# A list scheduler with PSUM banks owned by one engine at a time, four h banks in the last block, and low words of the weights scaled on ScalarE

## The chip, the cores and the metric

The kernel runs on one core of one Trainium2 chip. The core has five engines with queues of their own: TensorE (PE in the rows; PEld is its weight load), VectorE (DVE), ScalarE (ACT), GpSimd (POOL) and SyncE (SP). The metric is the device time of one execution in microseconds (us); smaller is better.

## What is computed

Banded attention over 4 batches, 8 heads, 576 positions and a head width of 64 feeds two multilayer perceptrons, each 512 to 2048 to 512 over 2304 tokens. Cut to what matters, the reference is:

```python
scores = np.where(mask, scale * q @ k.T + bias, -1e9)      # mask: 0 <= i - j < 128
attn = softmax(scores)
x = attn @ v                                              # 2304 x 512
h = x @ w_in
P = a[0] + a[1]*h + a[2]*h*h + a[3]*h*h*h
Q = 1 + abs(b[0])*abs(h) + abs(b[1])*h*h
x = (P / (Q + 1e-6)) @ w_out                              # first perceptron
h = x @ w2_in
return (h * (1 / (1 + np.exp(-h)))) @ w2_out              # second perceptron
```

## The kernel before

All data lie transposed, features on the partitions and tokens along the free axis. Products of fp32 are made as three matmuls of high and low parts: hi x hi, hi x lo and lo x hi. So each operand comes as a pair (xh and xl, gh and gl, the two parts of w and wo), of which the high part is a rounded copy ("cast", L447 on ScalarE, L451 on VectorE, L455 on GpSimd) and the low part a subtraction (L462 on VectorE, L466 on GpSimd).

**Weights.** The weights lie in DRAM as 64-bit floats. Each of 64 raw weight tiles (16 each of w1, wo1, w2 and wo2) is loaded as pairs of 32-bit words and made into fp32 by three operations on 128x512: an activation on the top words (L541, ScalarE), a shift of the low words to the right by 29 bits (L543, VectorE), and a shift-and-or of both (L545, VectorE).

**First stage, to about 551 us.** The 18 token tiles of 128 are worked in five blocks of 4, 4, 3, 4 and 3 tiles. There are 80 steps, one for each block and each of 16 hidden slices f. Blocks 0 and 1 run first with f 0 to 9 (block 0, then block 1), then with f 10 to 15; blocks 2, 3 and 4 follow whole. A step makes h in one PSUM bank by 12 matmuls (L844 to L846, in two halves), then evaluates the rational function on it: |h| and a linear form on ScalarE (L860, L866), den on VectorE (L874), its absolute value on ScalarE (L877), the numerator on VectorE (L878, L879), logarithm and exponential on ScalarE (L881, L883; the exponential is written back into the h bank), and three more operations on VectorE (L885, L887, L889). L889 is the last to read the h bank. Then come gh and gl, and 12 matmuls into four accumulators, acc0 to acc3 (L913 to L915), which run two steps behind (LAG 2). There are two h banks, four acc banks and two banks for the attention, atA and atB: eight in all.

The attention runs in 20 groups (5 blocks x 4 pairs of heads) between those steps: scores (L674, PE), mask (L680) and maximum (L687) on VectorE, exponential (L691, ScalarE), normalisation (L716 on ScalarE in block 0, L710 on GpSimd later), transposes (L730, PE), copies ph of the transposes out of PSUM (ScalarE, or GpSimd at L760, or VectorE at L767 and L771), and the product with v (L799, PE), whose result is split into xh and xl (L811) and is the block's input.

Beside this run the sums and splits of the second perceptron's weights (sums_w, sums_wo, st_w, st_wo), and spills of block 0's split weights to DRAM, which later blocks load again.

**Second stage, from about 551 us.** The second perceptron is computed in three groups of six token tiles with seven products in place of eight. Phase A (L1183 to L1185) makes h and the SiLU, phase B (L1249 to L1251) the output. Phase A's inputs are seven forms of x (xf; sums xs of 128x768), which are made during phase B of the group before (xf, xs at L462 or L466). Phase B's inputs xh_b and xl_b are made of g as it runs.

**Order.** Nothing here is ordered by hand. Each operation is recorded with a priority, one or more engines that may take it, and a cost (`Plan.op`); `Plan.schedule` is a list scheduler that simulates the engines and emits the program in the order that it found. `OPT` holds the options and priority offsets, `SHIFTS` a table (first operation, count, offset) that shifts priorities. `LATENCY` is the planner's time between an operation's end on one engine and its use on another. GpSimd and those VectorE operations that have no PSUM operand share a `port` in the plan. While PE has nothing to do at the program's start, dummy matmuls ("spin", L491) fill the planned gap.

## Time and profile before

| | us |
|---|---|
| median of 3 runs | 917.33 (916.65 to 919.83) |
| profiled execution | 920.78 |
| its span in the trace | 918.7 |

| engine | busy us | share of the span | instructions |
|---|---|---|---|
| PE | 875.1 | 95% | 5072 |
| DVE | 700.7 | 76% | 1382 |
| POOL | 618.9 | 67% | 591 |
| ACT | 583.5 | 64% | 1253 |

The span is what the trace covers; the execution's own time is 2.1 us longer. An engine's busy share is an average over stages with different limits, so the rows below go by stage. In the rows of a timeline the columns are start and duration in us, engine, line, operation, output<-inputs, sizes, count, and in brackets the idle time ahead of it with what ended it. In the groups by line, the numbers behind the first bar are total busy us and mean ns of one, behind the second the idle us ahead and what ended it.

### The profile page before, as it was taken

What the parts mean: (1) busy time and instruction counts of PE and PEld (TensorE: products, weight loads), DVE (VectorE), ACT (ScalarE), POOL (GpSimd) and SP (SyncE); (2) the same over time, 40 slices, a digit from 0 to 9 for tenths busy, and PEclk for the clock granted to TensorE, in tenths of its full rate; (3) what the DMA queues carried; (4) which work ended last, traced back from release to release, by engine and by line L of the source; (5) the groups of instructions that cost most, each with busy time, mean ns of one, the idle gap of its engine ahead of it and who ended that gap; (6) DMA issues with size and microseconds to landing.
All of it is one profiled execution on the core that took longest, in us unless ns stands there. A gap on an engine that the chain in (4) does not pass through costs nothing.

```text
span 918.7 us, 15313 instructions
## 1 busy us (share of the span) xinstructions
PE 875.1 (95%) x5072; PEld 769.7 (84%) x5072; DVE 700.7 (76%) x1382; ACT 583.5 (64%) x1253; POOL 618.9 (67%) x591
## 2 busy tenths in 40 slices
PE   8879899999999999999998999999999999999998
PEld 6647667877777888777777989999899998999998
DVE  5789988789999989999998985449843389533662
ACT  5878888689887788878777775336323365233441
POOL 2255655454767779778788776559954499645895
PEclk8989999999999999999999999999999999999999
DMA  7645585367798879757796888988788898788884
GB/s 238 252 133 165 197 273 165 137 199 275 234 340 260 252 243 307 243 192 239 239 345 221 286 266 303 325 296 285 239 279 256 264 307 256 250 270 253 249 269 167
DMA packets 80606, 228.94 MB, mean 249 GB/s; under 512 B 8464, under 2 KB 17168, under 8 KB 80528
## 3 DMA queue, kind: packets, MB, share of 16 engines
q1 hardware_dynamic: 78224, 219.58, 73.3%
q10 hardware_dynamic: 2304, 8.39, 2.3%
q8 instruction: 40, 0.66, 0.3%
q14 instruction: 38, 0.31, 0.1%
HBM read 178.65 MB, written 49.28 MB: 248 GB/s over the span
## 4 chain that ended last, share of the span: by engine, by line
PE 55%; DVE 15%; POOL 10%; ACT 10%; DMA 6%; issue 3%; SPq 0%; POOLq 0%; ACTq 0%; DVEq 0%
PE h L844 4%; PE z_a L1183 4%; PE z_a L1185 4%; PE z_a L1184 4%; PE h L845 3%; PE h L846 3%; POOL xf L466 3%; DVE t L874 3%; PE acc L913 3%; PE acc L915 2%; PE acc L914 2%; ACT t L866 2%; PE z_b L1249 2%; PE z_b L1251 2%; PE z_b L1250 2%
## 5 line engine op out<-in xcount | busy, mean ns | idle before, releaser
L913 PE MATMUL acc<-gh,wo 128*128 128x512 f32 (+1 forms) x320 | 121.4, 379 | 1.0 <-ACT x L447 0.8
L915 PE MATMUL acc<-gl,wo 128*128 128x512 f32 (+1 forms) x320 | 118.3, 370 | 2.7 <-POOL gl L466 2.6
L914 PE MATMUL acc<-gh,wo 128*128 128x512 f32 (+1 forms) x320 | 118.1, 369 | 0.4 <-POOL wo L466 0.4
L447 ACT CAST xh_b<-g 128x384 fp32r<-128x384 f32 x137 | 68.5, 514 | 78.7 <-PE z_b L1251 36.2
L462 DVE TENSOR_TENSOR xl_b<-g,xh_b 128x384 fp32r<-128x384 f32 x75 | 99.3, 1364 | 22.3 <-ACT xh_b L447 19.0
L466 POOL TENSOR_TENSOR gl<-t,gh 128x512 fp32r<-128x512 f32 (+1 forms) x80 | 98.5, 1231 | 22.6 <-ACT gh L447 15.6
L466 POOL TENSOR_TENSOR xl_b<-g,xh_b 128x384 fp32r<-128x384 f32 x93 | 107.6, 1172 | 3.8 <-ACT xh_b L447 1.2
L844 PE MATMUL h<-xh,ws 128*128 128x512 f32 (+1 forms) x256 | 97.0, 379 | 11.3 <-DVE t L889 11.2
L846 PE MATMUL h<-xh,ws 128*128 128x512 f32 (+1 forms) x256 | 93.0, 363 | 0.0
L845 PE MATMUL h<-xl,ws 128*128 128x512 f32 (+1 forms) x256 | 92.9, 363 | 0.0
L366 ACT ACTIVATE g<-t_a 128x384 f32<-128x384 f32 x72 | 37.8, 525 | 84.2 <-DVE t_a L359 84.2
L874 DVE SCALAR_TENSOR_TENSOR t<-t,ab,h 128x512 f32<-128x512 f32 (+1 forms) x80 | 55.3, 691 | 22.6 <-ACT t L866 20.0
L913 PEld LDWEIGHTS acc<-gh,wo 128*128 128x128 f32 x320 | 60.1, 188 | 13.8 <-issue 4.5
L915 PEld LDWEIGHTS acc<-gl,wo 128*128 128x128 f32 x320 | 60.1, 188 | 11.7 <-POOL gl L466 4.1
L844 PEld LDWEIGHTS h<-xh,ws 128*128 128x128 f32 x256 | 48.0, 188 | 25.3 <-DVE t L889 17.9
L466 POOL TENSOR_TENSOR g<-g,g 128x384 f32<-128x384 f32 x57 | 64.6, 1142 | 3.9 <-DVE xl_b L462 1.5
L914 PEld LDWEIGHTS acc<-gh,wo 128*128 128x128 f32 x320 | 60.1, 188 | 8.1 <-POOL wo L466 1.5
L860 ACT ACTIVATE t<-h,ab 128x512 f32<-128x512 f32 (+1 forms) x80 | 51.2, 641 | 23.4 <-PE h L846 22.9
L691 ACT ACTIVATE e<-e,m 128x128 f32<-128x128 f32 x144 | 56.2, 391 | 13.8 <-DVE m L687 13.5
L1183 PE MATMUL z_a<-xf,w2s 128*128 128x384 f32 x192 | 64.2, 334 | 0.4 <-DVE t L889 0.4
L1249 PE MATMUL z_b<-xh_b,wo2s 128*128 128x384 f32 x192 | 64.1, 334 | 0.0
L1251 PE MATMUL z_b<-xh_b,wo2s 128*128 128x384 f32 x192 | 64.1, 334 | 0.0
(178 smaller groups left out, 2736.1 us busy)
## 6 DMA issues: line engine op xcount, KB each, us to landing
w2s<-forms_w SPq DMA_DIRECT2D x84, 512.0 KB, 4.5
wo2s<-forms_wo SPq DMA_DIRECT2D x84, 512.0 KB, 4.6
ws<-sc SPq DMA_DIRECT2D x64, 512.0 KB, 4.8
raw_w<-in_w SPq DMA_DIRECT2D x32, 512.0 KB, 4.9
raw_wo<-in_wo SPq DMA_DIRECT2D x32, 512.0 KB, 4.6
forms_w<-st_w SPq DMA_DIRECT2D x24, 512.0 KB, 5.5
...
```

Of the source, the lines that this page charges most:

```text
L462: nc.vector.tensor_tensor(out=o, in0=a, in1=b, op=op)
L466: nc.gpsimd.tensor_tensor(out=o, in0=a, in1=b, op=op)
L844: nc.tensor.matmul(o, lhsT=T[W][:, 0, c], rhs=xh, start=kt == 0, stop=False)
L845: nc.tensor.matmul(o, lhsT=T[W][:, 0, c], rhs=xl, start=False, stop=False)
L846: nc.tensor.matmul(o, lhsT=T[W][:, 1, c], rhs=xh, start=False, stop=kt == KD - 1)
L874: nc.vector.scalar_tensor_tensor(out=t("t1"), in0=t("t2"), scalar=ab[:, 0:1], in1=hp_(), op0=ALU.add, op1=ALU.mult)
L913: nc.tensor.matmul(a, lhsT=T[WO][:, 0, c], rhs=T[G1][:, :n], start=first_f, stop=False)
L914: nc.tensor.matmul(a, lhsT=T[WO][:, 1, c], rhs=T[G1][:, :n], start=False, stop=False)
L915: nc.tensor.matmul(a, lhsT=T[WO][:, 0, c], rhs=T[G2][:, :n], start=False, stop=last_f)
L1183: nc.tensor.matmul(o, lhsT=w(0, kt * P), rhs=x[:, 0, kt], start=st and kt == 0, stop=False, skip_group_check=True)
L1249: nc.tensor.matmul(o, lhsT=w(0, m * P), rhs=h, start=st and q == 0, stop=False, skip_group_check=True)
L1251: nc.tensor.matmul(o, lhsT=w(1, m * P), rhs=h, start=False, stop=q == NQ - 1, skip_group_check=True)
```

## The change

1. **The plan.** The scheduler keeps for each PSUM bank the last operation on it and its engine (`banks`, `last_in`); an operation of another engine on that bank starts no earlier than that one's end plus `LATENCY`. The shared port of GpSimd and VectorE has a free time for each of the two, and 60 ns in place of 120 may overlap. PE gets 110 ns more in the plan after an idle time. Costs of the score and AV matmuls and of the weights' activations rise.
2. **Low words.** The shift by 29 bits becomes a product with 2^-29 and a bias, an Identity activation on ScalarE that reads and writes the low words as integers (L548 of after).
3. **The last block.** In steps 64 to 79, h of every second pair of steps (g % 4 > 1) goes to atA and atB in place of the two h banks. The operation that opens the second stage's buffers no longer waits for operations on atA and atB.
4. **Options.** gl, the weights' lo parts, the first block's normalisation and the tables may be taken by one more engine each; most priority offsets are other numbers; `SHIFTS` has 22 entries in place of 69.

The matmuls of the computation are the same; of the 48 dummy ones 36 are left. By the order, VectorE has 64 shifts less and ScalarE 64 products more; of 32 casts of split weights (L447 on ScalarE before) 25 go to GpSimd; of 32 normalisations of the first block on ScalarE (128x128) 16 remain, and VectorE has 4 (128x512); of 80 gl GpSimd keeps 70 and VectorE gets 10; of gh ScalarE has 54 (46 before) and GpSimd 24 (33).

```diff
+LOW_SCALE = 2.0 ** -29 * (1.0 - 2.0 ** -21)
...
-    'gl': 'pool',
-    'whi': 'act',
-    'wlo': 'pool',
+    'gl': 'dve|pool',
+    'whi': 'act|pool',
+    'wlo': 'dve|pool',
...
-    'tabs': 'pool',
+    'tabs': 'act|pool',
...
-    'norm0': 'act',
+    'norm0': 'dve|act',
...
-    'gl0': 'pool',
-    'la': 8.923,
-    'lb': 10.6,
-    'dm2': 0.291,
+    'gl0': 'dve|pool',
+    'la': 11.218,
+    'lb': 11.925,
+    'dm2': 0.198,
...
-    'xlead': 7.017,
-    'slead': 1.6,
+    'pw2': 134.061,
+    'rw2': 3.246,
+    'pwo2': 213.504,
+    'rwo2': 0.354,
+    'xlead': 2.688,
+    'slead': 0.322,
+    'shift': 'act',
+    'tail': 1,
...
-    (4, 1, 0.56), (77, 2, -0.09), (103, 1, 0.11), (136, 3, -1.1), (139, 1, 1.03), (175, 2, -1.11), (178, 1, 0.2), (276, 6, -0.06), (388, 2, 0.39),
...
+    (2, 2, -1.42), (276, 9, 1.2), (550, 2, 0.55), (863, 26, 0.27), (1304, 54, 0.14), (1885, 52, 0.05), (1938, 8, 0.63), (2057, 7, -0.19),
...
+PORT_GAP = 60.0
+STALL = 110.0
...
-        psum = any(t[0] in ("h", "atA", "atB") or t[0].startswith("acc") for t in list(reads) + list(writes))
-        o.port = {e for e in o.alts if e == "pool" or e == "dve" and not psum}
+        o.banks = {t[:2] for t in list(reads) + list(writes) if t[0] in ("h", "atA", "atB") or t[0].startswith("acc")}
+        o.port = {e for e in o.alts if e == "pool" or e == "dve" and not o.banks}
...
-                when = lambda o: max(f, o.ready, landed[-8] if o.dma and len(landed) >= 8 else 0.0, port_free - 120 if eng in o.port else 0.0)
+                when = lambda o: max([f, o.ready, landed[-8] if o.dma and len(landed) >= 8 else 0.0, port_free["pool" if eng == "dve" else "dve"] - PORT_GAP if eng in o.port else 0.0]
+                                     + [last_in[k][1] + LATENCY[last_in[k][0], eng] for k in o.banks if k in last_in and last_in[k][0] != eng])
...
-                o.end = free[eng] = st + o.cost
+                o.end = free[eng] = st + o.cost + (STALL if eng == "pe" and st > free.get(eng, 0.0) + 20 else 0.0)
                 if eng in o.port:
-                    port_free = o.end
+                    port_free[eng] = o.end
+                for k in o.banks:
+                    last_in[k] = (eng, o.end)
...
+        nc.vector.memset(lnb[:, 2:3], 2.0 ** -18 - 0.5)
...
-            pl.op(p - 0.6, "act", c_act(NR), lambda: nc.scalar.activation(out=top(), in_=top(), func=AF.Prelu, scale=2.0 ** -112, alpha=2.0 ** 32),
+            pl.op(p - 0.6, "act", c_act(NR) + 45, lambda: nc.scalar.activation(out=top(), in_=top(), func=AF.Prelu, scale=2.0 ** -112, alpha=2.0 ** 32),
                   reads=[rk + (1,)], writes=[rk + (1,)])
-            pl.op(p - 0.5, "dve", c_dve2x(NR), lambda: nc.vector.tensor_scalar(
-                out=low(), in0=low(), scalar1=29, scalar2=None, op0=ALU.logical_shift_right), reads=[rk + (0,)], writes=[rk + (0,)])
+            pl.op(p - 0.5, any_of(OPT["shift"], {
+                "act": (c_act(NR) + 45, lambda: nc.scalar.activation(out=low(), in_=low(), func=AF.Identity, scale=LOW_SCALE, bias=lnb[:, 2:3])),
+                "dve": (c_dve2x(NR), lambda: nc.vector.tensor_scalar(
+                    out=low(), in0=low(), scalar1=29, scalar2=None, op0=ALU.logical_shift_right))}), 0, None, reads=[rk + (0,), ("lnb", 0)], writes=[rk + (0,)])
...
-            pl.op(pH, "pe", 120 + sum(c_pe4(P if k0[i] else 192) for i in half), s_mm, reads=[("kd", gi), ("qd", gi)], writes=list(S_))
+            pl.op(pH, "pe", 210 + sum(c_pe4(P if k0[i] else 192) for i in half), s_mm, reads=[("kd", gi), ("qd", gi)], writes=list(S_))
...
-        pl.op(pA, "pe", 200 + (n + sum(1 - k for k in k0)) * 215, av, reads=[("vh", gi), PH], writes=[AV])
+        pl.op(pA, "pe", 290 + (n + sum(1 - k for k in k0)) * 215, av, reads=[("vh", gi), PH], writes=[AV])
...
+        tail = OPT["tail"] and blk == nb1 - 1 and g % 4 > 1
-        Hk = ("h", g)
+        Hk = (("atA", "atB")[g % 2], f"h{g}") if tail else ("h", g)
-                T[Hk] = h_p.tile([P, 512], F32, tag="h", name=f"h{g}")
+                T[Hk] = banks[Hk[0]] if tail else h_p.tile([P, 512], F32, tag="h", name=f"h{g}")
...
-    last_att = [o for k, l in pl.tile_ops.items() if k[0] in ("kd", "qd", "vh", "e", "ph", "m", "l", "atA", "atB", "tab", "tabs") for o in l]
+    last_att = [o for k, l in pl.tile_ops.items() if k[0] in ("kd", "qd", "vh", "e", "ph", "m", "l", "tab", "tabs") for o in l]
```

On PE in the last block, the end of one step's h (three of its 12 matmuls) and what stands behind it, before:

```order
L844 MATMUL h_6063<-xh_3_5072,ws_15_5930 128x384
L845 MATMUL h_6063<-xl_3_5073,ws_15_5930 128x384
L846 MATMUL h_6063<-xh_3_5072,ws_15_5930 128x384
L913 MATMUL acc_0_0_5363<-gh_6061,wo_2304 128x384
L914 MATMUL acc_0_0_5363<-gh_6061,wo_2304 128x384
L915 MATMUL acc_0_0_5363<-gl_6073,wo_2304 128x384
L913 MATMUL acc_0_1_5392<-gh_6061,wo_2304 128x384
L914 MATMUL acc_0_1_5392<-gh_6061,wo_2304 128x384
L915 MATMUL acc_0_1_5392<-gl_6073,wo_2304 128x384
```

and after, where L851 to L853 are the lines of h:

```order
L851 MATMUL bank_atA<-xh_3_5082,ws_14_5819 128x384
L852 MATMUL bank_atA<-xl_3_5083,ws_14_5819 128x384
L853 MATMUL bank_atA<-xh_3_5082,ws_14_5819 128x384
L851 MATMUL bank_atB<-xh_0_4240,ws_15_5905 128x384
L852 MATMUL bank_atB<-xl_0_4241,ws_15_5905 128x384
L853 MATMUL bank_atB<-xh_0_4240,ws_15_5905 128x384
L851 MATMUL bank_atB<-xh_1_4550,ws_15_5905 128x384
L852 MATMUL bank_atB<-xl_1_4551,ws_15_5905 128x384
L853 MATMUL bank_atB<-xh_1_4550,ws_15_5905 128x384
```

Before, the accumulator matmuls of an earlier step stand between two steps' h; after, the h of two steps stand back to back in atA and atB, and between two uses of a bank lie 72 to 84 matmuls in place of 36.

On PE in the first attention groups, the last transposes (L730) and AV (L799) of one group, before:

```order
L730 MATMUL bank_atA<-ident,e_592 128x128 x2
L730 MATMUL bank_atB<-ident,e_592 128x128 x2
L799 MATMUL bank_atA<-ph_727,vh_448 64x256 x4
L799 MATMUL bank_atA<-ph_727,vh_448 64x128 x2
L799 MATMUL bank_atA<-ph_727,vh_448 64x256 x2
```

and after (L736 are the transposes; AV, L805, of this group comes later still):

```order
L736 MATMUL bank_atA<-ident,e_482 128x128 x2
L736 MATMUL bank_atB<-ident,e_482 128x128 x2
L851 MATMUL h_514<-xh_2_568,w_462 128x512
L852 MATMUL h_514<-xl_2_569,w_462 128x512
L853 MATMUL h_514<-xh_2_568,w_462 128x512
L851 MATMUL h_514<-xh_3_643,w_462 128x512
L852 MATMUL h_514<-xl_3_644,w_462 128x512
L853 MATMUL h_514<-xh_3_643,w_462 128x512
```

Before, AV stands right behind the transposes whose copies it reads; after, a half of a step's h stands behind the first transposes, and more of this kind behind the last.

On POOL near the end of the second stage's first phase B (xl2_b0_5_2 is a low part of group 0, round 5; xf and xs with _1 are the forms and sums for group 1), before:

```order
L466 TENSOR_TENSOR xf2_1_6744<-xf2_1_6744 128x768
L466 TENSOR_TENSOR xl0_b0_4_4_7159<-g0_9_6558,xh0_b0_4_4_7145 128x384
L466 TENSOR_TENSOR xf3_1_6943<-xs3_1_6929,xf3_1_6943 128x768
L466 TENSOR_TENSOR xs5_1_7196<-xf4_1_6767,xf5_1_6774 128x768
L455 TENSOR_SCALAR xf4_1_6767<-xf4_1_6767 128x768
L466 TENSOR_TENSOR xf4_1_6767<-xf4_1_6767 128x768
L466 TENSOR_TENSOR xf5_1_6774<-xs5_1_7196,xf5_1_6774 128x768
L466 TENSOR_TENSOR xl2_b0_5_2_7266<-g0_4_6374,xh2_b0_5_2_7216 128x384
L466 TENSOR_TENSOR xl3_b0_5_3_7280<-g0_6_6446,xh3_b0_5_3_7230 128x384
L466 TENSOR_TENSOR xl0_b0_5_4_7295<-g0_8_6523,xh0_b0_5_4_7239 128x384
L466 TENSOR_TENSOR xl2_b0_5_6_7308<-g0_12_6667,xh2_b0_5_6_7260 128x384
```

and after:

```order
L469 TENSOR_TENSOR xf0_1_6678<-xf0_1_6678 128x768
L469 TENSOR_TENSOR xl0_b0_6_0_7272<-g0_1_6214,xh0_b0_6_0_7254 128x384
L469 TENSOR_TENSOR xl2_b0_6_2_7291<-g0_5_6374,xh2_b0_6_2_7277 128x384
L469 TENSOR_TENSOR xf1_1_7089<-xs1_1_7044,xf1_1_7089 128x768
L469 TENSOR_TENSOR xl1_b0_6_5_7322<-g0_11_6592,xh1_b0_6_5_7310 128x384
L469 TENSOR_TENSOR xl2_b0_6_6_7337<-g0_13_6670,xh2_b0_6_6_7328 128x384
L469 TENSOR_TENSOR xl3_b0_6_7_7353<-g0_15_6751,xh3_b0_6_7_7331 128x384
L469 TENSOR_TENSOR xf2_1_6713<-xf2_1_6713 128x768
L469 TENSOR_TENSOR xf6_1_7365<-xs6_1_7348,xf6_1_7365 128x768
L469 TENSOR_TENSOR xf5_1_6743<-xs5_1_7385,xf5_1_6743 128x768
L458 TENSOR_SCALAR xh0_b1_0_0_7449<-g1_0_7447 128x384
```

Before, five operations on forms and sums of the next group and a cast stand ahead of the low parts of rounds 5 and 6; after, two stand among the low parts of round 6 and three behind its last.

## Rows read from the trace of the kernel before

**Rows 1.** Windows: us, busy PE, PEld, DVE, ACT, POOL (count), clock, DMA, GB/s.

```profile
0.00:36.00 36.00, 30.10 (x241) 23.71 (x242) 22.35 (x94) 23.14 (x82) 8.68 (x16) 0.91 0.66 217
36.00:80.00 44.00, 36.48 (x270) 24.14 (x271) 37.41 (x128) 35.17 (x110) 18.25 (x15) 0.92 0.54 188
80.00:485.00 405.00, 388.92 (x2195) 308.64 (x2192) 369.76 (x799) 326.01 (x676) 280.61 (x269) 1.00 0.73 241
485.00:551.00 66.00, 60.22 (x333) 57.00 (x332) 59.55 (x107) 51.41 (x96) 50.63 (x56) 1.00 0.79 257
551.00:610.00 59.00, 58.88 (x338) 58.58 (x339) 28.26 (x50) 25.43 (x51) 34.37 (x38) 1.00 0.89 304
```

**Rows 2.** Waits of PE: line, waited for, us in total, times, longest us.

```profile
PE h L844 <- DVE t L889: 14.9, 20, 2.1
PE bank_atA L799 <- POOL ph L760: 5.3, 2, 3.2
PE bank_atA L1250 <- POOL xl_b L466: 4.1, 2, 2.0
PE bank_acc L674 <- DMA qd<-in_qn: 2.9, 1, 2.9
```

**Rows 3.** Timeline of PE: matmuls behind a wait in the first stage.

```profile
490.13 0.45 PE L844 MATMUL h<-xh,ws 128*128 128x384 f32 x1 [2.13 <-DVE t L889]
...
298.79 0.44 PE L844 MATMUL h<-xh,ws 128*128 128x384 f32 x1 [1.53 <-DVE t L889]
...
98.78 0.44 PE L799 MATMUL bank_atA<-ph,vh 128*64 128x256 f32 x2 [2.12 <-POOL ph L760]
...
60.93 0.65 PE L799 MATMUL bank_atA<-ph,vh 128*64 128x256 f32 x3 [3.23 <-POOL ph L760]
```

**Rows 4.** Timeline of ACT, DVE and POOL in one step of the last block.

```profile
521.46 0.58 ACT L860 ACTIVATE t<-h,ab 128x384 f32<-128x384 f32 x1
...
522.64 0.61 DVE L874 SCALAR_TENSOR_TENSOR t<-t,ab,h 128x384 f32<-128x384 f32 x1 [0.17 <-ACT t L866]
...
527.30 0.55 DVE L889 SCALAR_TENSOR_TENSOR t<-t,h 128x384 f32<-128x384 f32 x1
...
528.47 1.02 POOL L466 TENSOR_TENSOR gl<-t,gh 128x384 fp32r<-128x384 f32 x1
```

**Rows 5.** Groups by line, shapes kept apart.

```profile
L543 DVE TENSOR_SCALAR raw_wo<-raw_wo 128x512 uint32<-128x512 uint32 x32 | 18.2, 567 | 2.1 <-DMA raw_wo<-in_wo 2.1
L543 DVE TENSOR_SCALAR raw_w<-raw_w 128x512 uint32<-128x512 uint32 x32 | 16.3, 514 | 0.0
L541 ACT ACTIVATE raw_w<-raw_w 128x512 f32<-128x512 f32 x32 | 21.3, 672 | 4.9 <-DMA raw_w<-in_w 4.6 <-issue 0.3
L447 ACT CAST w<-raw_w 128x512 fp32r<-128x512 f32 x16 | 10.4, 660 | 1.9 <-PE h L846 1.9
L716 ACT ACTIVATE e<-e,l 128x128 f32<-128x128 f32 x32 | 9.9, 388 | 1.8 <-DVE l L703 1.7
L462 DVE TENSOR_TENSOR xl_b<-g,xh_b 128x384 fp32r<-128x384 f32 x75 | 99.3, 1364 | 22.3 <-ACT xh_b L447 19.0 <-POOL xh_b L455 2.8
L359 DVE TENSOR_TENSOR t_a<-t_a,bank_atA 128x384 f32<-128x384 f32 x36 | 19.9, 554 | 38.4 <-PE bank_atA L1185 38.4
```

**Rows 6.** Timeline of PE: matmuls behind a wait at the joints of the second stage.

```profile
660.25 0.69 PE L1250 MATMUL bank_atA<-xl_b,wo2s 128*128 128x384 f32 x1 [2.02 <-POOL xl_b L466]
...
781.50 0.44 PE L1250 MATMUL bank_atA<-xl_b,wo2s 128*128 128x384 f32 x1 [2.03 <-POOL xl_b L466]
```

**Rows 7.** Windows of 5 us around these joints, columns as in Rows 1.

```profile
655.00:660.00 5.00, 3.19 (x17) 2.54 (x15) 5.00 (x5) 1.23 (x3) 5.00 (x3) 1.00 0.62 179
660.00:665.00 5.00, 4.75 (x19) 4.75 (x20) 3.16 (x3) 0.00 (x0) 5.00 (x6) 0.66 0.63 224
...
775.00:780.00 5.00, 4.24 (x23) 3.59 (x21) 5.00 (x5) 2.48 (x6) 4.92 (x4) 1.00 0.57 197
780.00:785.00 5.00, 3.50 (x13) 3.21 (x14) 4.44 (x4) 0.00 (x0) 5.00 (x4) 0.80 0.79 249
```

**Rows 8.** Timeline of POOL ahead of the first joint.

```profile
656.38 2.15 POOL L466 TENSOR_TENSOR xf<-xs,xf 128x768 fp32r<-128x768 f32 x1
```

37 lines of the change are left out of this document (17 added, 20 removed), and 10 rows, old and new, of the table SHIFTS.

## Prediction

> **What bounds the kernel now.** I first read the busy time of each engine by stage [rows 1]. TensorE issues from start to end; the reader is to see where it does not. In the second multiplication's first half (551 to 610 us) 338 matmuls of 128x384 stand in 59.00 us, one in 174.6 ns, and this is the pace without a loss. Everywhere else I count what is missing against it: 5.9 us without TensorE work in 0 to 36, 7.5 us in 36 to 80, 16.1 us in 80 to 485, and in 485 to 551, where 333 matmuls should take 58.1 us, 7.9 of the 66.0 us. So the bound is TensorE's work plus the holes in it, and a schedule can only win back holes: the matmuls are the same before and after (only 12 of 48 dummy ones at the start go).
>
> Second I read what ended those holes [rows 2]: 20 waits of the h product for the last VectorE reader of an h bank (L889; 14.9 us), two of the attention's AV product for GpSimd's copy of the transposes (5.3 us), two of the second multiplication for low parts made by GpSimd (4.1 us), one for a load (2.9 us). VectorE is busy for 369.76 of 405 us in the block stage (91%), ScalarE for 326.01 (80%), GpSimd for 280.61 (69%) [rows 1].
>
> **Last block's h in four banks.** In 485 to 551 us TensorE stands before L844 until L889 has let go of the bank [rows 3], 2.13 us at 490. One step of this block [rows 4]: ScalarE's first operation starts at 521.46 right behind its h matmuls, the den product starts at 522.64, L889 ends at 527.85 and GpSimd's gl at 529.49, so the bank is held for 6.5 us behind the matmuls and g is ready after 8.1 us. By the order, TensorE had 6.3 us of matmuls between a bank's last matmul and the next use of it (36 of 174.6 ns), less than 6.5, with nothing to spare for a queue; now it has 12.5 to 14.5 us. The distance from h to its first acc matmul also grows, from 8.3 to 9.3-10.4 us, against 8.1 needed. Both waits should be gone, so the 7.9 us are nearly all at stake. The last step's chain is still waited for in part, since nothing but acc work is left then: I take **-7**. Bounds: -10, were waits of the block's steps before 485 to go as well (one like 490.13 and a little more); -3, if VectorE, busy for 59.55 of 66.00 us [rows 1], becomes what limits the steps: its work there then has to fit the rest, and less of the hole closes. The opening of the second multiplication's buffers no longer waits for the two attention banks; were it to, it would wait to the block's end, so nothing is won or lost there.
>
> **Low words by ScalarE.** 64 shifts of 567 and 514 ns [rows 5] leave VectorE (32 x 0.567 + 32 x 0.514 = 34.6 us), 64 activations come to ScalarE. The same shape in the neighbouring activation takes 672 ns [rows 5], so +43 us; 25 casts of weights leave it for GpSimd (x 0.660 = 16.5 us) and 16 products of the first block's normalisation go (x 0.388 = 6.2 us) [rows 5]; 14 form casts that go and 8 gh casts that come I take to cancel. That is +20 us for ScalarE up to 551, -34 for VectorE, and some +15 for GpSimd, my estimate for 25 casts at a little under the 0.66 us they took. Were all of it in the block stage (80 to 485), they would be busy for 346, 335 and 296 of 405 us: 85, 83 and 73%. The product is off the chain of its weights (they are loaded steps ahead) but on ScalarE's queue: behind it wait the five activations of an h step, behind these L889, behind that TensorE's next h. It also stands ahead of ScalarE's spills of the weights to DRAM, which are read much later. That VectorE has 34 us less shortens the same chain, as six of its steps are VectorE's. Of the 14.9 us on L889 about half lie in the block stage (the longest is the 1.53 us at 298.79 [rows 3]), and a shorter chain closes these; the AV wait of 2.12 us at 98.78 [rows 3] goes too, since more matmuls now stand behind the transposes. Against that come ScalarE's products. I take **-3**: the AV wait and 1 us net. Bounds: -12 (all but 4 of the 16.1) and +9 (each of the 20 waits in rows 2 grows by one product of 0.67 us, +13.4, less 4).
>
> A rule speaks against this edit: the Trainium skill, "ScalarE: Activation LUTs", section "Rules for kernel authors", wants adds and multiplies on VectorE, not on ScalarE. The rows agree on the instruction (0.51 to 0.57 us against 0.67); by the rule the edit would cost 64 x 0.13 = 8 us of engine time, and were all of that on the path, the sum below would be 12 instead of 20 us smaller than the time before.
>
> **A bank belongs to one engine at a time in the plan.** The chip behaves so already: the den product at 522.64 waited 0.17 us for L866, though it reads only what L860 wrote and the bank [rows 4]; L866 reads the same bank. The planner did not know it. Now the planned times of a step are nearer to those of the trace, and what it puts between dependent operations grows. In the first attention groups the TensorE work between the transposes and AV goes, by the order, from 0.0, 0.8, 2.1, 0.8, 0.0 us to 1.5, 2.4, 4.5, 1.5, 2.1. At 60.93 TensorE waited 3.23 us [rows 3] for this with 0.0 behind it; with 2.1 there, 2.1 of it close. From 0 to 80 us 13.4 us of TensorE's time are empty [rows 1], 2.9 of it a load [rows 2] that nothing here moves. I take **-4**: the 2.1 and as much again over the other four groups. Bounds: -8 (10.5 less one chain of 2.5 us at the start that nothing can fill), +4 (seven of the products come among ScalarE's first 45 instructions, ahead of the exponentials; six of them on the path, 6 x 0.67).
>
> **The joints of the second multiplication.** At 660.25 and 781.50 TensorE waited 2.0 us for low parts from GpSimd [rows 6], and around it ran short: in these four windows of 5 us stand 72 matmuls where 4 x 28.6 = 114 would, 42 x 0.1746 = 7.4 us [rows 7]. The granted clock is 0.66 and 0.80 there, a mean of the two levels (1.2 and 2.4 GHz), after the windows in which TensorE stood. Ahead of the awaited xl_b GpSimd did the next group's sums of x, 2.15 us each [rows 8]: by the order five of these and a cast lay in front of the last two rounds of low parts, and now only two, with three behind the last low part and VectorE taking four more after its own. So the awaited parts come some 6.5 us (3 x 2.15) earlier and both waits go. What is late next is the forms themselves: the next half needs seven of them, one each 1.04 us from its start, and three of 2.1 us on GpSimd and four on VectorE, side by side, take some 6 to 8 us against the 6.2 us in which they fall due. I take **-6**, as the last ones can be late by a microsecond at one joint or both. Bounds: -7.4 and 0.
>
> **Sum.** -7 - 3 - 4 - 6 = -20 against the profiled execution: span 918.7 to 898.7, with 2.1 us around it 900.8. That execution was 3.45 us above the median of the runs, 917.33, and I apply the same sum to the median: 917.3 - 20 = **897.3 us**.
>
> **Rivals.**
> R1, the joints only move: the seven forms are not ready when the next half starts. VectorE's xl_b takes 1364 ns where an operation of the same size with an input in PSUM takes 554 ns [rows 5], so VectorE and GpSimd are slow when both work from SBUF, as they would on these forms; TensorE stands at the start of the half, and the clock falls there instead. The joint's 6 us are lost: 917.3 - 14 = 903.3. For it: the forms are now later by the order. Against: in the half that follows GpSimd has 34.37 of 59.00 us of work and VectorE 28.26 [rows 1].
> The Trainium skill has a rule for this: "Perfetto Trace Analysis", section "Optimizing Scalar/DVE Operations", says that VectorE and GpSimd share a port, so that moving work between the two might not help; the 1364 ns agree with it.
> R2, ScalarE's queue eats the middle: the prologue gives nothing, 8 of the 20 waits on L889 grow by 0.67 us (+5.4): 917.3 - 7 - 6 + 5.4 = 909.7. For it: ScalarE does five of the chain's steps and has the most added. Against: VectorE, with six steps of the chain, loses 34 us of work where ScalarE gains 20.
> R3, slower: ScalarE becomes the bound of the block stage. At 80% it has no cover for 64 more products that come in bursts with the weights; if 32 of them delay the h chain and TensorE by 0.67 us each, +21.4 in place of the -7 of prologue and middle: 917.3 - 13 + 21.4 = 925.7. It decides from 19 delays of 64 on (13 / 0.67), 24 for more than the margin. For it: TensorE's waits on L889 are already the longest list; against: 85% is still below VectorE's 91% of before, and ScalarE's part of a step is 5 x 0.6 = 3 us of the 4.2 us (24 x 174.6 ns) that TensorE takes even for the narrowest blocks.
> R4, nothing: the plan is nearer to the chip but the holes only change places, 917.
>
> **Chances.** Forecast 0.60, R1 0.12, R2 0.12, R3 0.10, R4 0.06. Range: R1 and R2 with a little above R2's 909.7, up to 912; below, the sum of all lower bounds is -37 (880), of which I take a good half of what lies beyond the forecast, so 885 (-32). The upper bounds together (+10) are R3, which with R4 and about 0.04 of the rest stays outside. About 0.3% (2.75 us) is what a measurement can tell from no change; faster by more 0.84, within 0.06, slower 0.10.
>
> **What would show it.** Right: in the last block the waits on L889 sum to under 1 us, and the block's 333 matmuls fit into about 59 us. At the two joints no wait on xl_b over 0.5 us and a granted clock near 1.00 in the windows of the last low parts; R1 shows as waits of L1190 (the first half's matmul) on the forms. The block stage between the first group and block 4 loses 13 us rather than 16; R2 and R3 show as more than 15 us of waits on L889 that VectorE got from ScalarE, with the product L548 just ahead on ScalarE. In the first 80 us TensorE's empty time goes from 13.4 to about 9. Wrong altogether: if the three stages' times change by less than 2 us each, or if the product takes well over 0.67 us.

## The result, and the profile of the changed kernel

The changed kernel takes 885.69 us (median of 4 runs, 883.01 to 890.59) against 918.58 (916.65 to 921.41, now of 4 runs too) for the kernel before: a ratio of 0.9646, with a 95% interval of 0.9595 to 0.9696. The forecast was 897.3 with a range of 885 to 912. The direction was right and the time lies at the range's lower edge: the change is worth 33 us where I had added up 20. The profiled execution took 885.54 us, its span is 883.8.

The windows of the changed kernel, columns as in [rows 1]:

```profile
0.00:36.00 36.00, 30.95 (x272) 22.89 (x274) 29.31 (x129) 27.25 (x100) 9.27 (x16) 1.00 0.71 228
36.00:80.00 44.00, 37.06 (x260) 25.74 (x255) 36.44 (x107) 36.35 (x96) 27.84 (x25) 0.84 0.58 204
80.00:457.00 377.00, 369.02 (x2101) 297.35 (x2100) 334.44 (x724) 326.77 (x671) 270.97 (x277) 1.00 0.75 250
457.00:524.00 67.00, 66.23 (x371) 64.17 (x370) 60.37 (x105) 59.75 (x113) 56.70 (x60) 1.00 0.80 273
...
627.50:632.50 5.00, 5.00 (x31) 5.00 (x30) 3.36 (x5) 2.45 (x5) 4.88 (x5) 1.00 0.96 292
632.50:637.50 5.00, 5.00 (x31) 5.00 (x30) 4.65 (x4) 2.57 (x5) 5.00 (x4) 1.00 0.89 321
```

The last two windows are the place of the first joint (the matmul that waited at 660.25 before starts at 632.55 here): TensorE stands no more (5.00 of 5.00 busy), and the granted clock is 1.00 where it was 0.66 [rows 7]. In the block stage VectorE's share is now 334.44 of 377 us (89%, 91% before) and ScalarE's 326.77 (87%, 80% before): the two are level. From 36 to 80 us the granted clock is lower than before, 0.84 against 0.92.

The waits of TensorE in the changed kernel, which answer to [rows 2] (L851 is L844 of before, L896 is L889, L805 is L799, L922 is L915):

```profile
PE h L851 <- DVE t L896: 5.7, 8, 2.0
PE bank_atA L680 <- DVE xl L817: 2.3, 3, 1.4
PE bank_atA L680 <- DVE m L693: 2.0, 1, 2.0
PE bank_atA L805 <- POOL ph L766: 1.6, 1, 1.6
...
PE acc L922 <- POOL gl L469: 0.5, 1, 0.5
```

The waits for the h bank fell from 14.9 to 5.7 us, those of AV from 5.3 to 1.6, and the wait for xl_b is gone.

To see in which stage the time went, I take three places that every kernel has: the first matmul of h in the last block, the first of the second stage, and the last of all. In the timeline of TensorE, before:

```profile
471.89 0.44 PE L844 MATMUL h<-xh,ws 128*128 128x384 f32 x1
...
551.02 0.41 PE L1183 MATMUL z_a<-xf,w2s 128*128 128x384 f32 x1 [0.40 <-DVE t L889]
...
914.99 0.34 PE L1251 MATMUL bank_atB<-xh_b,wo2s 128*128 128x384 f32 x1
```

and after:

```profile
456.63 0.33 PE L851 MATMUL h<-xh,ws 128*128 128x384 f32 x1
...
524.10 0.33 PE L1190 MATMUL z_a<-xf,w2s 128*128 128x384 f32 x1
...
880.08 0.34 PE L1258 MATMUL bank_atA<-xh_b,wo2s 128*128 128x384 f32 x1
```

The way to the last block got 15.3 us shorter, the last block 11.6 (79.1 to 67.5), the second stage 8.0 (364.0 to 356.0). That is 34.9 us, the whole difference of the two spans. The stages do not hold quite the same work, though: with four banks 36 accumulator matmuls stand behind the first matmul of the second stage, with two banks 24. These 12 more take 2.1 us at the 174.6 ns of one, and they count in the second stage in place of the last block. For like work the last block got 9.5 us shorter and the second stage 10.1.

In the last block alone, TensorE's waits before (first fence) and after (second):

```profile
PE h L844 <- DVE t L889: 5.4, 8, 2.1
PE acc L915 <- POOL gl L466: 2.0, 1, 2.0
```

```profile
PE acc L922 <- POOL gl L469: 0.5, 1, 0.5
PE h L851 <- DVE t L896: 0.3, 1, 0.3
```

And in the groups by line, the product on the low words (L548) and VectorE's low parts, which answer to [rows 5]:

```profile
L465 DVE TENSOR_TENSOR xl_b<-g,xh_b 128x384 fp32r<-128x384 f32 x76 | 77.9, 1031 | 30.6 <-ACT xh_b L450 29.7
...
L548 ACT ACTIVATE raw_w<-raw_w,lnb 128x512 uint32<-128x512 uint32 x32 | 24.5, 766 | 0.0
L548 ACT ACTIVATE raw_wo<-raw_wo,lnb 128x512 uint32<-128x512 uint32 x32 | 24.4, 762 | 0.0
```

The product takes 0.764 us, not the 0.67 of its neighbour. VectorE's xl_b takes 1031 ns and not 1364.

### The profile page after: what moved, and what is told of

The parts are those of the page before. It is cut to its first block, busy times and chain, and to the rows that moved or that the text cites. A ratio compares the mean times of both kernels' runs of the same rounds, so it can differ in the third digit from the quotient of the medians.

```text
span 883.8 us, 15249 instructions
## 1 busy us (share of the span) xinstructions
PE 859.6 (97%) x5048; PEld 765.7 (87%) x5048; DVE 662.2 (75%) x1333; ACT 601.2 (68%) x1271; POOL 618.5 (70%) x611
## 4 chain that ended last, share of the span: by engine, by line
PE 74%; DMA 7%; ACT 6%; DVE 5%; POOL 5%; issue 2%; SPq 0%; ACTq 0%; POOLq 0%; DVEq 0%
PE h L851 5%; PE acc L920 5%; PE acc L922 5%; PE acc L921 5%; PE h L852 5%; PE h L853 5%; PE z_a L1191 4%; PE z_b L1257 4%; PE z_b L1258 4%; PE z_a L1192 4%; PE z_b L1256 4%; PE z_a L1190 4%; DMA raw_w<-in_w 3%; PE bank_atA L805 2%; PE bank_atA L680 2%
## 5 line engine op out<-in xcount | busy, mean ns | idle before, releaser
L922 PE MATMUL acc<-gl,wo 128*128 128x512 f32 (+1 forms) x320 | 118.2, 369 | 0.5 <-POOL gl L469 0.5
L469 POOL TENSOR_TENSOR xl_b<-g,xh_b 128x384 fp32r<-128x384 f32 x92 | 104.1, 1137 | 9.9 <-ACT xh_b L450 6.4
L469 POOL TENSOR_TENSOR gl<-t,gh 128x512 fp32r<-128x512 f32 (+1 forms) x70 | 86.4, 1235 | 22.3 <-ACT gh L450 20.1
L465 DVE TENSOR_TENSOR xl_b<-g,xh_b 128x384 fp32r<-128x384 f32 x76 | 77.9, 1031 | 30.6 <-ACT xh_b L450 29.7
L851 PE MATMUL h<-xh,ws 128*128 128x512 f32 (+1 forms) x224 | 84.1, 376 | 2.5 <-DVE t L896 2.5
L853 PE MATMUL h<-xh,ws 128*128 128x512 f32 (+1 forms) x224 | 82.2, 367 | 0.0
L852 PE MATMUL h<-xl,ws 128*128 128x512 f32 (+1 forms) x224 | 82.1, 367 | 0.0
L922 PEld LDWEIGHTS acc<-gl,wo 128*128 128x128 f32 x320 | 60.1, 188 | 9.0 <-POOL gl L469 1.0
L892 DVE SCALAR_TENSOR_TENSOR t<-t,h 128x512 f32<-128x512 f32 (+1 forms) x72 | 45.8, 637 | 24.9 <-ACT h L890 24.5
L1190 PE MATMUL z_a<-xf,w2s 128*128 128x384 f32 x192 | 64.1, 334 | 0.0
L1191 PE MATMUL z_a<-xf,w2s 128*128 128x384 f32 x192 | 64.1, 334 | 0.0
L1192 PE MATMUL z_a<-xf,w2s 128*128 128x384 f32 x192 | 64.1, 334 | 0.0
L1257 PE MATMUL z_b<-xl_b,wo2s 128*128 128x384 f32 x192 | 64.1, 334 | 0.0
```

Of the source, the lines that this page charges most:

```text
L469: nc.gpsimd.tensor_tensor(out=o, in0=a, in1=b, op=op)
L851: nc.tensor.matmul(o, lhsT=T[W][:, 0, c], rhs=xh, start=kt == 0, stop=False)
L852: nc.tensor.matmul(o, lhsT=T[W][:, 0, c], rhs=xl, start=False, stop=False)
L853: nc.tensor.matmul(o, lhsT=T[W][:, 1, c], rhs=xh, start=False, stop=kt == KD - 1)
L922: nc.tensor.matmul(a, lhsT=T[WO][:, 0, c], rhs=T[G2][:, :n], start=False, stop=last_f)
L1190: nc.tensor.matmul(o, lhsT=w(0, kt * P), rhs=x[:, 0, kt], start=st and kt == 0, stop=False, skip_group_check=True)
```

## The experiments

Four kernels have one part of the change alone, six are the changed kernel with one part undone, two try its numbers. Each group was measured beside the kernel before on its own chip, so ratios to the kernel before are compared. The stages are read as above, from one profiled execution of each; between a kernel with two banks and one with four, 2.1 us of the last block's and of the second stage's difference are the 12 matmuls. Kernels whose orders are the same up to the last block (before, E6 and E9; after, E2 and E5) reach it at times up to 3.8 us apart, so a stage's difference below 4 us says nothing by itself.

The joints can be read more finely. Without the accumulators' matmuls the second stage has 2016 on TensorE, six parts of 336. The third and the fifth part take 58.24 us in every kernel, and the second and the fourth hold the joints: the last column is what these two take beyond 116.5 us.

| kernel | ratio to before (95%) | last block starts | last block | second stage | lost at the joints |
|---|---|---|---|---|---|
| before | 1 | 471.9 | 79.1 | 364.0 | 9.7 |
| after | 0.9646 (0.9595 to 0.9696) | 456.6 | 67.5 | 356.0 | 0.4 |
| E6, before with four banks | 0.9931 (0.9903 to 0.9958) | 468.2 | 75.8 | 364.9 | 8.6 |
| E7, before with products on ScalarE | 1.0190 (1.0171 to 1.0208) | 483.1 | 86.3 | 364.6 | 9.5 |
| E8, before with the bank rule | 0.9982 (0.9958 to 1.0006) | 468.6 | 81.6 | 364.8 | 8.9 |
| E9, before with late forms | 1.0039 (1.0014 to 1.0064) | 471.2 | 81.2 | 367.1 | 12.0 |
| E1, after, shifts on VectorE in place | 0.9847 (0.9821 to 0.9874) | 474.5 | 70.9 | 357.9 | 0.4 |
| E11, after, shifts on VectorE, planned | 0.9799 (0.9756 to 0.9842) | 461.0 | 71.1 | 363.2 | 2.9 |
| E2, after with two banks | 0.9702 (0.9673 to 0.9731) | 460.4 | 74.9 | 355.4 | 0.4 |
| E3, after without the bank rule | 0.9775 (0.9729 to 0.9821) | 465.2 | 72.9 | 358.7 | 0.4 |
| E4, after with the old port | 0.9699 (0.9670 to 0.9728) | 457.3 | 69.2 | 361.4 | 4.9 |
| E5, after with early forms | 0.9673 (0.9646 to 0.9700) | 457.9 | 69.1 | 360.5 | 5.0 |
| E12, after with the old numbers | 0.9861 (0.9817 to 0.9905) | 471.7 | 68.4 | 360.8 | 3.2 |
| E13, after without a table of shifts | 0.9705 (0.9653 to 0.9756) | 463.2 | 68.8 | 359.0 | 2.5 |

### One part alone, in the kernel before

**E6, four banks.**

```diff
+        tail = blk == nb1 - 1 and g % 4 > 1
-        Hk = ("h", g)
+        Hk = (("atA", "atB")[g % 2], f"h{g}") if tail else ("h", g)
...
-                T[Hk] = h_p.tile([P, 512], F32, tag="h", name=f"h{g}")
+                T[Hk] = banks[Hk[0]] if tail else h_p.tile([P, 512], F32, tag="h", name=f"h{g}")
```

> The kernel before with one part of the change, h of every second pair of steps of the last block in atA and atB (and the opening of the second stage no longer behind those banks). Up to the last block the orders are the same. Theory (the bank's holding time of 6.5 us against 36 matmuls set the pace of the last block): the block, from its first h to the first matmul of phase A, goes from 79.1 us to 68 to 70, near the 67.5 of the changed kernel, the waits for L889 there from about 7 us to under 1, and the whole gets 9 to 11 us shorter. Rival (VectorE, 34 us shorter by the shifts, is what let the block run): with all shifts still on VectorE the block stays at 76 us or more and the whole gains under 3 us.

The ratio is 0.9931, some 6 us. In the profile 3.7 us of it lie ahead of the last block, where the orders are the same, and the block shrank by only 3.3 us, 1.2 of like work. TensorE's waits in the block (L845 is h, L914 and L916 the accumulators), and the block's window, columns as in [rows 1]:

```profile
PE acc L916 <- POOL gl L466: 4.1, 7, 1.6
PE acc L914 <- POOL gh L455: 1.0, 2, 0.6
PE h L845 <- DVE t L890: 0.6, 1, 0.6
PE acc L914 <- ACT gh L447: 0.5, 1, 0.5
```

```profile
468.15:543.90 75.75, 69.45 (x373) 64.31 (x372) 68.92 (x117) 57.25 (x108) 58.53 (x59) 1.00 0.75 258
```

The wait for the bank is gone as forecast (5.4 to 0.6 us), but the next thing in the chain is late in its place: gl and gh, 2.0 us before and 5.6 now. That is not GpSimd's doing. gh starts 0.12 us behind L890 and gl 0.39 us behind gh in mean, as before (0.11 and 0.37); what comes late is L890. VectorE is busy for 68.92 of the block's 75.75 us (91%), and ScalarE waits 11.0 us for VectorE's den there (6.9 before). So the rival is not refuted. The bank wait went with all shifts still on VectorE, but the block stayed near the rival's 76 us; as these rows read, VectorE's work fills it. In the changed kernel VectorE has 60.8 us of work in the block, and with the shifts back on VectorE (E1 and E11 below) the block takes 70.9 and 71.1 us in place of 67.5.

**E7, products on ScalarE,** at the shifts' places in the old order.

```diff
-            pl.op(p - 0.5, "dve", c_dve2x(NR), lambda: nc.vector.tensor_scalar(
-                out=low(), in0=low(), scalar1=29, scalar2=None, op0=ALU.logical_shift_right), ...)
+            pl.op(p - 0.5, "dve", c_dve2x(NR), lambda: nc.scalar.activation(out=low(), in_=low(), func=AF.Identity, scale=LOW_SCALE, bias=lnb[:, 2:3]), ...)
```

> The kernel before with the low words scaled on ScalarE at the very place where the shifts stood; planned order otherwise the same. VectorE loses about 34 us, ScalarE gets 64 x 0.76 = 49 us. Theory 1 (VectorE at 91% is what lengthens the h chain): the stretch from 80 us to the last block gets 4 to 8 us shorter, waits for L889 fall from 14.9 to about 9. Theory 2 (ScalarE's queue is what the chain feels): waits for L889 grow, whole 3 to 10 us longer. If it changes by less than 2 us, neither engine's share was what mattered.

This part alone makes the kernel 1.9% slower, 18 us, twice the upper bound that I gave it. Neither engine is overfull: in the block stage VectorE and ScalarE are each busy for some 345 of 403 us (86%), less than VectorE's 91% before.

```profile
80.00:483.00 403.00, 382.60 (x2153) 301.78 (x2152) 345.13 (x747) 344.70 (x714) 266.56 (x260) 1.00 0.69 233
```

What it costs stands in the timeline at one place that both kernels have. First before, ScalarE and VectorE, just ahead of the wait at 490.13 [rows 3]:

```profile
486.38 0.82 ACT L447 CAST xf<-xf 128x768 fp32r<-128x768 f32 x1
487.10 0.83 ACT L447 CAST xf<-xs 128x768 fp32r<-128x768 f32 x1
...
488.31 0.66 ACT L866 ACTIVATE t<-h,na 128x384 f32<-128x384 f32 x1
```

```profile
489.00 0.61 DVE L874 SCALAR_TENSOR_TENSOR t<-t,ab,h 128x384 f32<-128x384 f32 x1 [0.23 <-ACT t L866]
489.53 0.55 DVE L889 SCALAR_TENSOR_TENSOR t<-t,h 128x384 f32<-128x384 f32 x1
```

then E7, the same with TensorE's wait (all lines are one or two higher; L545 is the product):

```profile
499.89 0.82 ACT L448 CAST xf<-xf 128x768 fp32r<-128x768 f32 x1
500.61 0.76 ACT L545 ACTIVATE raw_wo<-raw_wo,lnb 128x512 uint32<-128x512 uint32 x1
501.27 0.81 ACT L448 CAST xf<-xs 128x768 fp32r<-128x768 f32 x1
...
502.47 0.66 ACT L867 ACTIVATE t<-h,na 128x384 f32<-128x384 f32 x1
```

```profile
503.16 0.61 DVE L875 SCALAR_TENSOR_TENSOR t<-t,ab,h 128x384 f32<-128x384 f32 x1 [0.87 <-ACT t L867]
503.69 0.55 DVE L890 SCALAR_TENSOR_TENSOR t<-t,h 128x384 f32<-128x384 f32 x1
```

```profile
504.29 0.44 PE L845 MATMUL h<-xh,ws 128*128 128x384 f32 x1 [3.25 <-DVE t L890]
```

The product stands on ScalarE between two casts and puts off what follows by 0.66 us; VectorE waits for L867 in L875, of the next step, 0.64 us longer than before (0.87 against 0.23); L890 of the step before, whose bank TensorE wants, stands behind L875 on VectorE; and the wait at this place grows from 2.13 to 3.25 us. The product explains some 0.65 of these 1.12 us; the rest was not followed. VectorE had room and could not use it. Over the whole kernel the waits of h on L890 went from 14.9 to 23.8 us. This is the prediction's rivals R2 and R3, as a mechanism, and in the old order it is real.

**E8, the bank rule.**

```diff
-                when = lambda o: max(f, o.ready, ...)
+                when = lambda o: max([f, o.ready, ...] + [last_in[k][1] + LATENCY[last_in[k][0], eng] for k in o.banks if k in last_in and last_in[k][0] != eng])
```

> The kernel before with the one rule in its planner that a bank is one engine's at a time; options, costs and the table of shifts stay, so the whole first stage is planned anew by numbers that were fitted without the rule. Theory (a plan nearer to the chip puts more work between dependent operations): the waits for L889 fall from 14.9 us to 8 or less and the first stage gets 4 to 8 us shorter; the joints stay as they are. Rival (the numbers and the rule belong together): the first stage gets no shorter, or up to 6 us longer, with waits in other places.

No change that can be measured (0.9982). The rival holds: the waits for the h bank stay (below, L893 is L889), and the numbers and the rule belong together.

```profile
PE h L848 <- DVE t L893: 14.3, 16, 2.1
```

**E9, late forms.**

```diff
-    'xlead': 7.017,
-    'slead': 1.6,
+    'xlead': 2.688,
+    'slead': 0.322,
```

> The kernel before with two numbers changed, the lead of the forms of x (xlead 7.017 to 2.688, slead 1.6 to 0.322). TensorE's order is the same in every row; only which engine makes the forms, and when, differs, in the second stage. Theory (forms ahead of the low parts made TensorE stand at the two joints): the waits for xl_b of 2.0 us go, the clock stays at 1.00 there, and the whole gets 6 to 8 us shorter, with VectorE's xl_b of about 1360 ns as before in mean. Rival 1 (the forms then come late): waits of L1183 on xf of 2 us or more at each joint, gain under 3 us. Rival 2 (the planner's new port, which alternates VectorE and GpSimd, is what shortened the low parts from 1364 to 1031 ns and so closed the joints): waits for xl_b of 1 us or more stay.

Here my theory fell. The wait for xl_b went, as forecast, and the kernel still became 0.4% slower. Neither rival names what came. TensorE waits at each joint for longer than before, one row earlier: 3.78 us at the first and 3.76 at the second, where it was 2.0, with no releaser named ("issue").

```profile
669.96 0.41 PE L1249 MATMUL bank_atA<-xh_b,wo2s 128*128 128x384 f32 x1 [3.78 <-issue]
```

VectorE's timeline names it:

```profile
661.22 8.18 DVE L462 TENSOR_TENSOR xl_b<-g,xh_b 128x384 fp32r<-128x384 f32 x5
669.32 0.54 DVE L1269 TENSOR_TENSOR v<-v,bank_atA 128x384 f32<-128x384 f32 x1
```

The matmul opens the last of the seven products in bank atA; the addition L1269 empties that bank, ends at 669.86, and stands behind five low parts that took 8.18 us on VectorE, 1.6 each, while GpSimd worked on forms and low parts of its own. At the second joint the same rows stand in the same order, and the matmul again starts 0.10 us behind the end of L1269. So the joint's limit is the work of VectorE and GpSimd from SBUF together, and moving the forms alone only changes which piece of it is late. (The expectation for E5 below speaks of a weight load here; that was a first reading, which this row corrects.)

### One part undone, in the changed kernel

**E1 and E11, the low words back on VectorE.** E1 leaves every other row where it stands:

```diff
-                "act": (c_act(NR) + 45, lambda: nc.scalar.activation(out=low(), in_=low(), func=AF.Identity, scale=LOW_SCALE, bias=lnb[:, 2:3])),
+                "act": (c_act(NR) + 45, lambda: nc.vector.tensor_scalar(
+                    out=low(), in0=low(), scalar1=29, scalar2=None, op0=ALU.logical_shift_right)),
```

E11 sets one option, and the plan is made anew:

```diff
-    'shift': 'act',
+    'shift': 'dve',
```

> The changed kernel with the low words shifted on VectorE again, at the very place where the products stand; TensorE's, GpSimd's and SyncE's orders are the same in every row. ScalarE loses 64 x 0.76 = 49 us, VectorE gains some 35. Theory (with the product alone the kernel before became 1.9% slower, because it was put where ScalarE had no room, so place and engine belong together): here the shifts fall on places where VectorE has no room, and the whole gets 5 to 15 us longer, in the first stage. Rival (ScalarE's work is a plain loss, the change gains in spite of it): the whole gets 5 us shorter or more.

> The changed kernel with the low words shifted on VectorE and the plan made anew for it, where the earlier run kept the order and lost 18 us. Theory 1 (VectorE's share is the bound of the first stage): the plan can't make up for it, VectorE is at 93% again, and the whole is 8 to 15 us longer than the changed kernel. Theory 2 (only the fit of place and engine matters): with a plan of its own the shift on VectorE costs less than 4 us.

E1 is 2.0 points of the ratio behind the changed kernel (18 us). In the profile the last block starts 17.9 us later, and 5.3 us more are lost behind that. So an order made for one engine loses 18 us when the 64 operations go to the other, in both directions (E7 and E1). VectorE is busy for 93% of the stretch, and the waits for the h bank are nearly those of before again (14.9 us in 20 waits there):

```profile
80.00:474.50 394.50, 376.89 (x2125) 299.50 (x2124) 367.82 (x783) 305.26 (x634) 276.98 (x279) 1.00 0.72 240
```

```profile
PE h L852 <- DVE t L897: 12.5, 19, 1.7
```

In E11, planned for VectorE, the whole is 1.5 points behind (14 us), so the product is worth having. But only 4.4 us of this stand ahead of the last block, with VectorE at 353.00 of 381 us (93%) and only 3.7 us of waits on the h bank in that stretch. 3.6 us stand in the last block and 7.2 in the second stage.

```profile
80.00:461.00 381.00, 374.66 (x2124) 299.32 (x2125) 353.00 (x781) 303.28 (x630) 262.70 (x265) 1.00 0.72 242
```

In the groups of VectorE at the second stage's beginning, E11 (532 to 601 us) has five of the weights' shift-and-or operations still to do,

```profile
L551 DVE SCALAR_TENSOR_TENSOR raw_wo<-raw_wo 128x512 uint32<-128x512 uint32 x5 | 4.1, 818 | 0.4
```

and the changed kernel (524 to 588 us) two:

```profile
L551 DVE SCALAR_TENSOR_TENSOR raw_wo<-raw_wo 128x512 uint32<-128x512 uint32 x2 | 1.6, 816 | 0.2 <-ACT raw_wo L548 0.2
```

Here the plan answers a fuller VectorE by putting off some of the second perceptron's weights, and TensorE then loses time in a stage that had no hole: 4.7 us in the second stage's first part, with 2.5 us of waits for VectorE's additions that empty the banks (L362), and 2.5 us at the joints. That the put-off weights cause the first of these fits the rows and was not tried by itself. Theory 1 holds in the sum, not in the place that it named. The offsets of E11 were not fitted to it, so 14 us is the product's worth in this plan, not its worth at best.

**E2, two banks.**

```diff
-    'tail': 1,
+    'tail': 0,
```

> The changed kernel with two h banks in the last block; up to that block all orders are the same. Theory (the two further banks are worth most when gl and the rest of the chain keep up): the last block goes from 67.5 us to 75 to 79, the whole gets 8 to 11 us longer. Rival (the new plan makes the chain short enough for two banks): the block stays under 71 us, the whole within 3 us.

The last block goes from 67.5 to 74.9 us, at the lower end of what the theory gave (2.1 of it the 12 matmuls), the whole gets 5 us longer by ratio, less than the theory's 8 to 11, and the waits for the block's banks come back:

```profile
PE h L851 <- DVE t L896: 3.9, 7, 1.2
```

With E6 this is a table of four. From the first h of the last block to the last matmul of all, so that the 12 matmuls count on both sides, two banks take 443.1 and four 440.7 us in the old plan, 430.3 and 423.5 in the new. The banks are worth 2.4 us in the one and 6.8 in the other; banks and plan together give more than the sum, since with the banks free VectorE's work sets the block, and the new plan has less of it there. By ratio, E2 is 0.6 points behind the changed kernel, and the intervals still touch; it is the block's own time and waits that carry the verdict.

**E3, without the bank rule.**

```diff
-                when = lambda o: max([f, ...] + [last_in[k][1] + LATENCY[last_in[k][0], eng] for k in o.banks if k in last_in and last_in[k][0] != eng])
+                when = lambda o: max([f, ...])
```

> The changed kernel without the plan's rule that a bank is one engine's at a time; everything else stays, the plan is made anew. Alone, in the kernel before, the rule was worth 3 us up to the last block and nothing in all. Theory (the rule carries the gain of the first stage once the numbers fit it): the last block starts 8 to 12 us later than the 456.6 of the changed kernel, the whole gets 8 to 15 us longer. Rival (the rule is a detail; balance of the engines carries the gain): the whole gets less than 4 us longer.

1.3 points behind (12 us), and the last block starts 8.5 us later: the theory's numbers. The h waits are at 12.5 us in 12 waits again:

```profile
PE h L850 <- DVE t L895: 12.5, 12, 1.9
```

So the rule is worth nothing alone and up to 12 us with the numbers that were fitted to it. Up to, because the offsets were not fitted anew without the rule: as in E11, a part of the 12 us may be that misfit, and no run tells the two apart.

**E4, the old port, and E5, early forms.** E4 replaces the port's free time (L274 of after); E5 sets `xlead` and `slead` to the old 7.017 and 1.6.

```diff
-port_free["pool" if eng == "dve" else "dve"] - PORT_GAP if eng in o.port else 0.0
+max(port_free.values()) - 120 if eng in o.port else 0.0
```

> The changed kernel with the planner's old port, one free time for GpSimd and VectorE and 120 ns of overlap; the rest of the plan's rules and numbers stay, and the plan is made anew from the first stage on. Theory (the joints are open because VectorE and GpSimd are kept from queueing on each other): VectorE's xl_b goes from 1031 ns towards 1350, waits at the joints of 2 us or more come back, 5 to 9 us longer in the second stage. Rival (the port's model matters little, the offsets do): xl_b stays under 1100 ns, the joints stay open, and only the first stage differs, by up to 5 us either way.

> The changed kernel with the lead of the forms of x as before (xlead 2.688 to 7.017, slead 0.322 to 1.6); the first stage is the same up to the last block, the second differs. In the kernel before the reverse of it did not close the joints: there a weight load came late, which stood behind a store of v on SyncE, which waited for VectorE. Theory (early forms push low parts and v back on VectorE and GpSimd): 2 to 4 us at each of the two joints, 4 to 8 us longer. Rival (the forms' place does not matter, in either kernel): within 2 us.

The old port costs nothing up to the last block (457.3) and 5.4 us in the second stage, 4.5 of them at the joints; its ratio, 0.5 points behind, has an interval that touches that of the changed kernel. VectorE's xl_b goes to 1185 ns, less than half of the way back to 1364, and one wait of 2 us is back at the first joint, though not the two of before:

```profile
L465 DVE TENSOR_TENSOR xl_b<-g,xh_b 128x384 fp32r<-128x384 f32 x78 | 90.2, 1185 | 28.1 <-ACT xh_b L450 21.2 <-POOL xh_b L458 6.7
```

```profile
643.83 0.41 PE L1256 MATMUL bank_atB<-xh_b,wo2s 128*128 128x384 f32 x1 [1.96 <-ACT xf L450]
```

Early forms cost 4.5 us in the second stage by the profile, all of it at the joints (2.6 at the first, 2.0 at the second), with waits for VectorE's xl_b again, the longest at 639.61. The ratios alone can't tell E5 from the changed kernel (0.9673 and 0.9646, intervals that overlap), so it is the joints that speak for the theory.

```profile
639.61 0.44 PE L1257 MATMUL bank_atA<-xl_b,wo2s 128*128 128x384 f32 x1 [1.02 <-DVE xl_b L465]
```

Late forms cost 2.3 us at the joints with the old rules (E9) and win 4.6 with the new ones (E5 against after).

### The numbers

**E12, the mechanisms with the old numbers, and E13, without the table.** E12 has the changed kernel's code with `OPT` and `SHIFTS` of the kernel before (and the product and the four banks on). E13 has an empty `SHIFTS`:

```diff
-SHIFTS = [
-    (2, 2, -1.42), (276, 9, 1.2), (550, 2, 0.55), (863, 26, 0.27), (1304, 54, 0.14), (1885, 52, 0.05), (1938, 8, 0.63), (2057, 7, -0.19),
...
+SHIFTS = []
```

> The changed kernel's rules, four banks and products, with the options, priority offsets and table of shifts of the kernel before. Theory 1 (the mechanisms carry the gain): 895 to 905 against 921 of the kernel before. Theory 2 (the numbers that fit the rules carry it; single parts in the old plan added up to a loss): 912 or more. The last block should take 76 us or less in both, as two further banks alone gave 75.8.

> The changed kernel with an empty table of shifts; rules, options and products stay. If the table only polishes, the whole gets 3 to 6 us longer, in the first stage; if the order is held up by it, 10 us or more.

E12 lies between its two theories: 1.4% faster than before, with the last block at 68.4 us. Its last block starts at 471.7 us, where it did before (471.9). So the mechanisms with the old numbers give nothing ahead of the last block, 10.7 us in it (8.6 of like work), and 3.2 in the second stage, where the loss at the joints falls from 9.7 to 3.2 us even with the old, early forms. The rest, 20 us by ratio, is the numbers: 15 ahead of the last block and 5 in the second stage, 2.8 of these at the joints. E13 shows that the table of shifts is a small part of that: 0.6 points (5 us), within the overlap of the intervals, with the last block 6.6 us later by the profile.

## Why the prediction was right, and where it was not

The sign, the four places and the range held; the sum was 13 us short. That the range held is in part luck: the time lies 0.7 us above its lower edge, and the largest part of the gain came by numbers fitted to the new rules, for which the prediction has no term. By its own steps:

- **Last block, -7, measured -11.6, or -9.5 for like work.** The mechanism is shown: with four banks the wait for L889 goes from 5.4 to 0.6 us (E6) or 0.3 (after). Two things failed. The step "both waits should be gone" was false for the banks alone: TensorE then waited 5.6 us for gl and gh, because VectorE did not finish the steps sooner, which is the reason that I had given for the bound of -3. And the term was too small for the whole change, because I counted the waits from 485 us on: the block began at 471.9, and its 79.1 us hold 12.1 us beyond the pace of its 384 matmuls, where I counted 7.9.
- **Low words, with the block stage, -3, and the prologue, -4: measured together -15.3.** The block stage's term was mis-sized most. The price of the product was 0.764 us and not 0.67. The step "a shorter VectorE shortens the chain" is not borne out: taken over steps 0 to 63, from the last h matmul of a step to the end of its L889 it takes 9.04 us on average before and 9.07 after, while the waits of TensorE fall. As far as these rows show, TensorE waits less because it has other work in that time, not because the chain is quicker. The product alone cost 18 us (E7), outside my bound of +9, by the way of R2 and R3; in a plan made for it, it is worth 14 (E11). I had weighed it by shares of busy time, and shares did not decide: 86% on both engines was 18 us slower than 91% and 80%. With the old numbers the mechanisms give 0.2 of the 15.3 us (E12). So they come by the numbers, none of which I could have priced from the rows of before, together with the rule and the product that the numbers were fitted to (E3, E11).
- **The bank rule.** "The planner did not know it" was right, and that it frees time by itself was wrong (E8). It works through the numbers fitted to it (E3, up to 12 us). "The chip behaves so already" says more than its row: the 0.17 us [rows 4] are a wait that the end of L866 ended, and no run here shows whether the chip or the program's own semaphores ask for it.
- **Prologue, -4.** TensorE's empty time went from 13.4 us to 12.0 in the first 80 us, not to about 9. But by then it had begun 528 matmuls where it had begun 510, and 72 of them were dummy ones where 96 were (a dummy is two rows of the trace): 42 more of the computation. Without the dummy ones it was busy for 56.8 us, 51.2 before. The gain of 5.6 us has about the size that I gave it, with work in the place of dummy matmuls and not in holes that closed. The waits of AV fell as forecast, over the whole kernel from 5.3 to 1.6 us.
- **Joints, -6, measured -9.3 at the joints** (the second stage's -8.0 holds the 12 more matmuls). That is beyond my bound of -7.4, which I took from four windows of 5 us. The place was right, and the step that carried the term failed alone: making the forms later removes the wait for xl_b and sets one for bank atA in its place (E9), because VectorE's low parts, at 1.6 us each there, hold up the additions that empty the bank. It takes the new port as well, for which the prediction has no term: the old one loses 4.5 us there and has VectorE's xl_b at 1.19 us in place of 1.03 (E4), and the new rules bring most of the gain even with early forms (E12, 9.7 to 3.2). Neither the banks, nor the product, nor the bank rule does that alone (E6, E7, E8: 8.6 to 9.5), which leaves the port by elimination; it was not tried alone. R1 was a fair rival in kind (the joint moves), wrong in place: it moved to the bank and not to the forms.

Alone, the four parts come to +1.4 points (E6 -0.7, E7 +1.9, E8 -0.2, E9 +0.4), and the whole change to -3.5. The prediction added terms, and the terms do not add.

The Trainium skill, "ScalarE: Activation LUTs", section "Rules for kernel authors", speaks against the product: it wants adds and multiplies on VectorE. E7 agrees with it, and the instruction is slower on ScalarE, 0.76 us against 0.54. E1 and E11 differ: with the other order, the same operations moved back to VectorE cost 18 us, and with VectorE at 93% in a plan made for that, ScalarE was the better place by 14 us.

What stays open: how much of the 15 us ahead of the last block belongs to the engines' lists in the options (casts of weights to GpSimd, gl to VectorE) and how much to the priority offsets. Neither was tried by itself, and neither were the 110 ns behind an idle time and the raised costs. Where the time was can be said. Of the 15.3 us, 7.5 are empty time of TensorE (27.5 us before and 20.0 after, up to the last block), 4.2 are dummy matmuls (96 rows with 15.4 us, 72 with 11.2), and 2.5 stand in the score matmuls, whose 544 rows take 36.6 us before and 34.1 after.
